# One kernel, one change: eleven instead of six outer products of the first large tile in seven inner ones, with a ring of three buffers for their weight sums and SyncE issuing their stores

## The chip, the cores and the metric

The kernel runs on one core of a Trainium2 chip. The metric is the time of one execution in microseconds (us), measured on the device. A core has TensorE (PE in the profile, with its weight loads as PEld), VectorE (DVE), ScalarE (ACT), GpSimd (POOL) and SyncE (SP), which here issues DMAs only. SPq, ACTq and so on are the engines' instruction queues where they issue a transfer or wait.

## The reference

In float32: an attention without softmax whose scores decay with the distance of the tokens, and a SwiGLU block on its output.

```python
B, H, S, D = 8, 8, 576, 64
scores = (1 / sqrt(D)) * (q @ k.transpose(0, 1, 3, 2))
gamma  = 1 - 2 ** (-5 - h)                           # one for each head h
ret    = (scores * (gamma ** (i - j) where i >= j else 0)) @ v
x      = ret.transpose(0, 2, 1, 3).reshape(B * S, H * D)     # 4608 tokens x 512
g, val = x @ w_gate, x @ w_val                       # 512 x 1536 each
out    = (g * sigmoid(g) * val) @ w_out              # 1536 x 512
```

## The kernel before, in words

**Tiles.** Five token tiles. Tile 0 has 512 tokens and uses plain matmuls (`up0`, `down0`, L853 and L864). Tiles 1 to 4 have 1024 tokens each; each goes through an up stage (`up_stage`, gate and value products, SiLU, hidden values) and a down stage (`down_step`, the product with `w_out`). The attention is cut into ticks, each for one pair of heads of one batch: SyncE loads q, k and v (L282, L287), VectorE transposes and decays (`kT` is one of its results), TensorE forms scores and states (L532, L559 among others), and the output lands transposed in `xs[n]`, the x of the tile. Ticks of the next tiles are mixed into the work of the current one. One load is issued by ScalarE, the last that is recorded before tile 1's up stage (`queue = nc.scalar if i == needed(1) - 3`).

**Fewer multiplications.** The up stage of a large tile goes by three quads `qd` of the hidden size. In each quad, x and the weights are cut 2 x 2, and the block product is formed by seven outer products instead of eight, from sums of blocks (Strassen-Winograd). They are worked in the order `SETS = (1, 2, 6, 7, 4, 5, 3)`. Each outer product is again a 2 x 2 block product and is worked in one of two ways. In the plain one (`whole_slot`) it takes eight inner products; pairs accumulate in PSUM, and four banks are read. In the other one (`slot`) it takes seven inner products and seven reads of a bank, and it needs four inner sums of x (`x_inner`) and four of the weights (`w_inner`). `PLAIN` lists the outer products that are plain, all of tile 1. One inner product is one *slot*: two matmuls of 128 x 256 in `multiply` (L1183), into one of four banks (A, B, C, E). Most reads are VectorE additions in `combine` (L1040), which also is the line of the sums of x and of weights, whichever engine makes them. The outer products 2, 4, 5 and 3 finish hidden values: four `finish` calls each, a SiLU on ScalarE (L1197) and a product (L1198).

**Tile 1** (`busy`) has a second duty: while it runs, GpSimd forms the sums of weights of all 21 outer products, outer (`w_outer`) and inner (`w_inner`). The inner sums go into one of three blocks of SBUF and are stored to `up_sets` in DRAM (L1116); SyncE stores the raw and outer blocks beside them (L1118, L1119). Tiles 2 to 4 fetch them from there (`fetch_one`) and work every outer product in seven. In tile 1, six of the 21 outer products (6 and 7 of each quad) are worked in seven and fifteen are plain: 15 x 8 + 6 x 7 = 162 slots. Its products of L1198 are on VectorE; those of the other large tiles are on GpSimd.

**Order.** Every engine runs its instructions in the order in which they are recorded; nothing reorders them later. In tile 1's up stage a table by hand, `later(at, ...)`, says ahead of which slot a sum or a store is recorded; two loads of q, k and v are recorded after slots 13 and 30, behind a wait of SyncE. The sums of quad 0 that are needed first (`early_sums`) are recorded at the end of tile 0: outer sums 5 and 7 of the weights, inner sums of 1, 2 and 7, and the outer sums of x.

**The output weights.** Their sums (26 operands in each of three quads) are made during tile 0 by `out_sums`: GpSimd for quads 0 and 1 (L886), VectorE for the last. Each operand is stored at once by SyncE (L954) to `dn_ops` in DRAM, and its buffer comes free when the store has read it. They are recorded in groups of three operands; a table in the plan of tile 0 says after which `up0(f)` how many groups follow. The loads of the coming ticks (`next_load`) are recorded between them:

```python
        if f in (7, 10, 11):
            plan.append(lambda t=tick_at[f]: next_load(t))
        for _ in range({7: 3, 10: 4, 11: 3}.get(f, 0)):
            ...
                plan.append(lambda group=groups.pop(0)[1]: group())
```

Of the kernel before, what the change touches and what calls it, by code (L numbers as in the profile page):

```python
# [17 lines left out]
ALU = mybir.AluOpType  # L18
# [88 lines left out]


SETS = (1, 2, 6, 7, 4, 5, 3)
PLAIN = {(1, qd, o) for qd in range(3) for o in (1, 2, 4, 5, 3)}  # L110


def terms(text):
# [18 lines left out]
def kernel(  # L132
# [32 lines left out]
    nc = tc.nc  # L165

    B, H, S, D = q.shape
    NT, DM = out.shape
    DF = moe_w_gate.shape[1]
    P = 128  # L170
# [8 lines left out]
    TB = TW // 4  # L179
    NF = DF // P  # L180
    NQ = NF // 4
# [31 lines left out]
    hid = arena[:, 0 : 3 * QW].rearrange("p (q h t x) -> p q h t x", q=NQ, h=4, t=4)  # L213
# [831 lines left out]
    def x_sets(n):  # L1045

        x = xs[n].rearrange("p (K k) (T t x) -> p T K k t x", k=2, T=2, t=2)
        block = lambda a: rest[:, a : a + 1024].rearrange("p (k t x) -> p k t x", k=2, t=2)
        sets = {1: x[:, 0, 0], 2: x[:, 0, 1], 4: x[:, 1, 1], 7: x[:, 1, 0], 5: block(4096), 6: block(5120), 3: block(x0_at)}
        spots = [rest[:, x0_at + 1024 + TB * i : x0_at + 1024 + TB * (i + 1)] for i in range(4)]  # L1050
        spots += [rest[:, sum_at + 1024 + TB * i : sum_at + 1024 + TB * (i + 1)] for i in range(2)]
        spots += [rest[:, dn_at + 4096 + TB * i : dn_at + 4096 + TB * (i + 1)] for i in range(12)]
        spots += [operands[:, 5376 + TB * i : 5376 + TB * (i + 1)] for i in range(3)]
        new = {o: spots[3 * m : 3 * m + 3] for m, o in enumerate((1, 2, 7, 4, 6, 3, 5) if n == 1 else (1, 2, 7, 4, 5, 3, 6))}
        aside = new[3][2]

        def outer_sums(o, eng):
            a, b, sign = {5: (7, 4, 1), 6: (5, 1, -1), 7: (1, 7, -1), 3: (2, 6, -1)}[o]
            return [lambda k=k: combine(eng, sets[o][:, k], sets[a][:, k], sets[b][:, k], sign) for k in range(2)]

        def inner_sums(o, eng):
            a, (s1, s2, s4) = sets[o], new[o]
            return [lambda: combine(eng, s1, a[:, 0, 1], a[:, 1, 1], 1),
                    lambda: combine(eng, s2, s1, a[:, 0, 0], -1),
                    lambda: combine(eng, aside if o == 1 else a[:, 0, 1], a[:, 0, 0], a[:, 0, 1], -1),
                    lambda: combine(eng, s4, a[:, 1, 0], s2, -1)]

        def put_back(eng):
            a = sets[1]
            return [lambda: combine(eng, a[:, 0, 1], a[:, 0, 0], a[:, 0, 1], -1)]  # L1070

        def view(o, i, qd):
            a, (s1, s2, s4) = sets[o], new[o]
            return {1: a[:, 0, 0], 2: a[:, 1, 0], 3: s4, 4: a[:, 1, 1], 5: s1, 6: s2, 7: aside if o == 1 and qd == 0 else a[:, 0, 1]}[i]

        return outer_sums, inner_sums, put_back, view, sets
# [17 lines left out]
    def w_sets(qd):  # L1094

        up = lambda n, k: w_up[:, qd, :, 2 * n : 2 * n + 2, k, :]
        sets = {1: up(0, 0), 2: up(0, 1), 7: up(1, 0), 3: up(1, 1), 5: hid[:, qd, 2:4, 0:2], 6: hid[:, qd, 0:2, 2:4], 4: hid[:, qd, 2:4, 2:4]}
        blocks = (rest[:, x0_at + 1024 : x0_at + 2048], extra_at(1536, 1024), extra_at(0, 1024))
        new = {o: blocks[b].rearrange("p (g j x) -> p g j x", g=2, j=4) for o, b in {6: 1, 1: 2, 7: 0, 4: 2, 2: 1, 5: 2, 3: 0}.items()}

        def outer_sums(o):
            out, a, b = {5: (5, 7, 1), 6: (6, 3, 5), 7: (7, 3, 7), 4: (4, 2, 6)}[o]
            return [lambda g=g: combine(nc.gpsimd, sets[out][:, g], sets[a][:, g], sets[b][:, g], -1) for g in range(2)]

        def inner_sums(o):
            z = lambda k, m: sets[o][:, :, m, k * P : (k + 1) * P]
            to = lambda j: new[o][:, :, j]
            return [lambda: combine(nc.gpsimd, to(1), z(0, 1), z(0, 0), -1),
                    lambda: combine(nc.gpsimd, to(0), z(1, 1), z(0, 1), -1),
                    lambda: combine(nc.gpsimd, to(2), z(1, 1), to(1), -1),  # L1110
                    lambda: combine(nc.gpsimd, to(3), z(1, 0), to(2), -1)]

        def store(o, new_ones):
            dst = up_sets[qd][SETS.index(o)]
            if new_ones:
                return [lambda: nc.gpsimd.dma_start(out=dst[:, 6 * P :], in_=new[o].rearrange("p g j x -> p (g j x)"))]  # L1116
            raw = dst[:, 0 : 6 * P].rearrange("p (g x) -> p g x", g=2)
            return [lambda: nc.sync.dma_start(out=raw[:, :, P:], in_=sets[o][:, :, 0]),  # L1118
                    lambda: nc.sync.dma_start(out=raw[:, :, 0:P], in_=sets[o][:, :, 1, P:])]  # L1119

        return sets, new, outer_sums, inner_sums, store

    def early_sums():

        x_outer = x_sets(1)[0]
        _, _, w_outer, w_inner, store = w_sets(0)
        p = [w_outer(5), w_inner(1) + store(1, True), w_outer(7), w_inner(2) + store(2, True), w_inner(7) + store(7, True)]
        v = [f for o in (5, 6, 3, 7) for f in x_outer(o, nc.vector)]
        return p, v

    def up_stage(n):

        busy, base = n == 1, used[0]
# [16 lines left out]
        def later(at, *fs):  # L1150
            after.setdefault(at, []).extend(fs)
# [39 lines left out]
        def finish(k, c):  # L1191
            qd, o = seq[k]
            (T, H), (t, h) = final[o], divmod(c - 11, 10)
            src = to(k, c)
            s = io[:, (silus[0] % 4) * TB : (silus[0] % 4 + 1) * TB]
            silus[0] += 1
            nc.scalar.activation(out=s, in_=src[:, 0:TB], func=AF.Silu)  # L1197
            (nc.vector if busy else nc.gpsimd).tensor_tensor(out=hid[:, qd, 2 * H + h, 2 * T + t], in0=src[:, TB : 2 * TB], in1=s, op=ALU.mult)  # L1198

        def made(k, c, at):  # L1200
            if seq[k][1] in final:
# [100 lines left out]
        if not busy:  # L1302
            begin = lambda k: begins[k]
            if n + 1 < NTILE:
                for i, f in enumerate(x_inner(2, nc.gpsimd)):
                    later(i, f)
                for i, f in enumerate(x_outer(7, nc.vector)):
                    later(8 + 2 * i, f)
            for k, o in enumerate((6, 7, 4, 5, 3)):
                for i, f in enumerate(x_inner(o, nc.gpsimd)):  # L1310
                    later(begin(k + 1) - (n + 1 == NTILE) * 3 + i, f)
            later(begin(6), *put_back(nc.gpsimd))
        else:
            for o, at in {6: 6, 7: 10}.items():
                for i, f in enumerate(x_inner(o, nc.gpsimd)):
                    later(at + i, f)
            for qd in range(NQ):
                at = begins[len(SETS) * qd]
                _, _, w_outer, w_inner, store = w_sets(qd)
                if qd:  # L1320
                    outers = {5: 0, 6: 2, 7: 8, 4: 14}
                    inners = {6: 4, 1: 10, 7: 15, 4: 22, 2: 29, 5: 33, 3: 37}
                else:
                    outers, inners = {6: 0, 4: 14}, {6: 2, 4: 18, 5: 27, 3: 37}
                for o, start in outers.items():
                    for i, f in enumerate(w_outer(o)):
                        later(at + start + i, f)
                for o, start in inners.items():
                    for j, f in enumerate(w_inner(o)):
                        later(at + start + j, f)  # L1330
                    later(at + start + 3, *store(o, True))
                for i, o in enumerate((1, 2, 3, 5, 6, 7, 4)):
                    for j, f in enumerate(store(o, False)):
                        later(at + (1, 2, 4, 5, 7, 13, 20)[i] + j, f)

        def go(at):
            for f in after.pop(at, ()):
# [5 lines left out]
            after_tick()  # L1343
            if at % (2 if busy else 3) == 1:
                part_on()
            if busy and at - begins[2 * len(SETS)] in (38, 40, 42):
                fetch_one()
            if at + 1 == len(slots):
                while waiting:
# [102 lines left out]
    for f in range(2, NF):  # L1452
# [7 lines left out]
                plan.append(end_transposes)  # L1460
        if f in (7, 10, 11):
            plan.append(lambda t=tick_at[f]: next_load(t))
        for _ in range({7: 3, 10: 4, 11: 3}.get(f, 0)):
            if f >= (7, 10, NF)[groups[0][0]]:
                if f + 1 == NF and more_places:
                    plan.append(lambda places=more_places[:4]: pool_places.extend(places))
                    more_places.clear()
                if len(groups) % 9 == 0:
                    plan.append(lambda qd=groups[0][0]: negate(qd))
                plan.append(lambda group=groups.pop(0)[1]: group())  # L1470
# [87 lines left out]
```

## Time and profile before

| | |
|---|---|
| time, median of 3 runs | 1034.03 us (1033.91 to 1036.57) |
| profiled execution: time, span | 1034.89 us, 1033.16 us |
| TensorE clock granted, mean | 0.997 |
| PE busy | 1009.1 us, 98% |
| PEld busy | 828.7 us, 80% |
| VectorE busy | 727.6 us, 70% |
| GpSimd busy | 557.4 us, 54% |
| ScalarE busy | 286.7 us, 28% |
| DMA | 194.38 MB, mean 188 GB/s |

By stretches of the span, busy us of each engine:

| from : to | PE | DVE | ACT | POOL | DMA share |
|---|---|---|---|---|---|
| 0 : 178.94 (to the first matmul of tile 1's up stage) | 164.30 | 125.59 | 82.11 | 69.30 | 0.93 |
| 178.94 : 337.26 (tile 1's up stage) | 153.66 | 125.06 | 42.39 | 105.64 | 0.69 |
| 337.26 : 1033.00 (the rest) | 691.11 | 476.90 | 162.22 | 382.47 | 0.58 |

How to read it: times in the profile are microseconds from the start of the span, of one execution. An engine's busy time leaves out register and branch instructions, semaphores, and the issuing of DMAs; where an engine issues DMAs, that time is in its queue's rows. A row `PE bankA L1183 <- DVE rest L1040` is idle time of PE ahead of a matmul into bankA, ended by a VectorE instruction of L1040.

### The profile page before, as it was taken

The page shows a single profiled execution, that of the slowest core. Times are in us where ns is not written, and L with a number is a line of the kernel's source. Part 1 is how long each engine was busy: PE and PEld are TensorE (multiplying, and loading weights), DVE is VectorE, ACT ScalarE, POOL GpSimd, SP SyncE. Part 2 cuts the span into 40 slices and gives each one's busy share as a digit, 9 for nine tenths or more (in the row PEclk, how much of TensorE's full clock was granted, in tenths as well). Part 3 has the DMA queues.
Part 4 walks back from the last instruction along what each step waited for, and adds up shares of the span by engine and source line. Part 5 has one row for each costly group of instructions (what it writes and reads, how often), then busy time and mean ns, then how long its engine had stood idle before and what let it go on. Part 6 is the DMA issues. An engine that isn't in the chain of part 4 may idle for free.

```text
span 1033.2 us, 21382 instructions
## 1 busy us (share of the span) xinstructions
PE 1009.1 (98%) x8356; PEld 828.7 (80%) x8356; DVE 727.6 (70%) x1212; ACT 286.7 (28%) x638; POOL 557.4 (54%) x603
## 2 busy tenths in 40 slices
PE   6999989998999999999999999999999999999998
PEld 4644445887888888888888888888888888888887
DVE  5488878587788766875768768858576668565744
ACT  4465532131242231123333111133220012333110
POOL 3402259867474216764657237765582486566625
PEclk9999999999999999999999999999999999999999
DMA  9999887856595887756558777443454554445553
GB/s 242 251 263 248 216 198 264 262 147 191 116 260 159 203 237 197 208 178 181 166 163 234 197 187 218 163 144 143 143 189 154 159 162 163 154 142 182 177 162 102
DMA packets 281612, 194.38 MB, mean 188 GB/s; under 512 B 212968, under 2 KB 251112, under 8 KB 281512
## 3 DMA queue, kind: packets, MB, share of 16 engines
q1 hardware_dynamic: 244088, 82.51, 32.9%
q10 hardware_dynamic: 33760, 99.10, 29.2%
q0 software_dynamic: 3664, 11.41, 3.0%
q8 instruction: 66, 1.08, 0.5%
q14 instruction: 34, 0.28, 0.1%
HBM read 154.04 MB, written 38.93 MB: 187 GB/s over the span
## 4 chain that ended last, share of the span: by engine, by line
PE 82%; DMA 7%; DVE 5%; SPq 2%; issue 1%; ACT 1%; POOL 1%; ACTq 0%; DVEq 0%; POOLq 0%
PE bankE L1183 11%; PE bankA L1183 11%; PE bankB L1183 10%; PE bankC L1183 10%; PE bankB L1374 7%; PE bankC L1374 7%; PE bankE L1374 7%; PE bankA L1374 6%; DVE rest L1040 2%; PE outer L1183 2%; PE inner L1183 2%; PE outer L532 1%; DMA v<-in_v_dram 1%; PE outer L559 1%; DMA dn<-rest 1%
## 5 line engine op out<-in xcount | busy, mean ns | idle before, releaser
L1040 POOL TENSOR_TENSOR rest<-rest 128x512 f32<-128x512 f32 (+1 forms) x141 | 150.4, 1078 | 156.6 <-DVE rest L1040 114.2
L1198 POOL TENSOR_TENSOR arena<-rest,io 128x256 f32<-128x256 f32 x144 | 105.7, 745 | 73.2 <-ACT io L1197 72.9
L1197 ACT ACTIVATE io<-rest 128x256 f32<-128x256 f32 x192 | 79.4, 417 | 219.6 <-DVE rest L1040 159.2
L1183 PE MATMUL bankA<-rest,arena 128*128 128x256 f32 x416 | 107.6, 384 | 4.1 <-DVE rest L1040 3.9
L1183 PE MATMUL bankB<-rest,arena 128*128 128x256 f32 x416 | 106.1, 380 | 0.1
L1040 DVE TENSOR_TENSOR rest<-bankB,rest 128x512 f32<-128x512 f32 x113 | 76.1, 682 | 38.5 <-PE bankB L1183 24.6
L1183 PE MATMUL bankE<-rest,arena 128*128 128x256 f32 x400 | 102.2, 380 | 0.3 <-issue 0.3
L1040 DVE TENSOR_TENSOR rest<-bankA,rest 128x512 f32<-128x512 f32 x106 | 71.5, 682 | 40.6 <-PE bankA L1183 21.0
L1040 DVE TENSOR_TENSOR rest<-bankE,rest 128x512 f32<-128x512 f32 x105 | 71.0, 684 | 38.7 <-PE bankE L1183 25.8
L1040 POOL TENSOR_TENSOR arena<-arena 128x256 f32<-128x256 f32 (+1 forms) x84 | 76.3, 929 | 34.7 <-PE bankC L1183 19.6
L1183 PE MATMUL bankC<-rest,arena 128*128 128x256 f32 x372 | 94.8, 380 | 0.1
L1183 PEld LDWEIGHTS bankA<-rest,arena 128*128 128x128 f32 x416 | 78.8, 191 | 17.1 <-issue 3.4
L1040 DVE TENSOR_TENSOR rest<-bankC,rest 128x512 f32<-128x512 f32 x103 | 69.7, 683 | 30.1 <-PE bankC L1183 12.6
L1183 PEld LDWEIGHTS bankB<-rest,arena 128*128 128x128 f32 x416 | 78.8, 190 | 11.6 <-DVE rest L1040 0.9
L1183 PEld LDWEIGHTS bankE<-rest,arena 128*128 128x128 f32 x400 | 75.3, 190 | 11.8 <-DVE rest L1040 0.8
L1183 PEld LDWEIGHTS bankC<-rest,arena 128*128 128x128 f32 x372 | 70.1, 190 | 10.8 <-DVE rest L1040 1.2
L886 POOL TENSOR_TENSOR rest<-rest 128x256 f32<-128x256 f32 x43 | 34.3, 822 | 74.3 <-DVE rest L407 38.8
L1374 PE MATMUL bankB<-arena 128*128 128x256 f32 x264 | 61.0, 381 | 0.0
L1374 PE MATMUL bankC<-arena 128*128 128x256 f32 x264 | 60.8, 380 | 0.0
L1374 PEld LDWEIGHTS bankC<-arena 128*128 128x128 f32 x264 | 50.0, 190 | 6.9
L1374 PEld LDWEIGHTS bankB<-arena 128*128 128x128 f32 x264 | 49.8, 190 | 6.9
L1374 PE MATMUL bankA<-arena 128*128 128x256 f32 x240 | 55.3, 380 | 0.0
(267 smaller groups left out, 1930.1 us busy)
## 6 DMA issues: line engine op xcount, KB each, us to landing
arena<-up ACTq DMA_DIRECT2D x63, 896.0 KB, 4.6
arena<-dn ACTq DMA_DIRECT2D x65, 384.0 KB, 3.7
arena<-dn SPq DMA_DIRECT2D x39, 384.0 KB, 3.4
dn<-rest SPq DMA_DIRECT2D x78, 128.0 KB, 1.8
out_dram<-rest SPq DMA_DIRECT2D x35, 256.0 KB, 3.1
qk<-in_q_dram SPq DMA_DIRECT2D x108, 72.0 KB, 2.8
qk<-in_k_dram SPq DMA_DIRECT2D x108, 72.0 KB, 3.5
up<-arena POOLq DMA_DIRECT2D x15, 512.0 KB, 4.3
```

Of the source, the lines that this page charges most:

```text
L532: m = nc.tensor.matmul(value(i, hl, c), s["v"][rows, at], ret[rows, c % 2 if whole(i) else hl, c // 2], start=start, stop=start, skip_grou ...
L559: nc.tensor.matmul(xr[half[hl]] if c + 1 == NC else value(i, hl, c), state[half[hl], c, :], s["qT"][half[hl], ts(c, L)], start=False, stop ...
L886: eng.tensor_tensor(out=dst, in0=srcs[0], in1=srcs[1], op=ALU.add if op[0] == "add" else ALU.subtract)
L1040: eng.tensor_tensor(out=out, in0=a, in1=b, op=ALU.add if sign > 0 else ALU.subtract)
L1183: m = nc.tensor.matmul(b[:, g * TB : (g + 1) * TB], w[:, g], x, start=(opens and g == 0), stop=True, skip_group_check=True)
L1197: nc.scalar.activation(out=s, in_=src[:, 0:TB], func=AF.Silu)
L1198: (nc.vector if busy else nc.gpsimd).tensor_tensor(out=hid[:, qd, 2 * H + h, 2 * T + t], in0=src[:, TB : 2 * TB], in1=s, op=ALU.mult)
L1374: nc.tensor.matmul(b[:, m * TB : (m + 1) * TB], lhs[:, qd, ts(m, P)], w[:, qd], start=(opens and qd == 0 and m == 0), stop=(qd == NQ - 1), ...
```

## The change

Each part changes only the order, the engine or the buffer of work, and five outer products of tile 1.

- `PLAIN`: five more outer products of tile 1 are worked in seven inner ones: product 2 of quad 0, and products 1 and 2 of quads 1 and 2. Six become eleven, 162 slots become 157.
- `x_sets`, `w_sets`: other buffers for the inner sums. The three blocks of weight sums are used in turn, one ring over all 21 products.
- `store`: SyncE issues the stores of the inner weight sums in place of GpSimd.
- `early_sums`: the inner weight sums of product 7 are no longer recorded ahead of the stage.
- `finish`: in tile 1, the hidden products of outer product 2 go to GpSimd.
- `up_stage`: new slots for the sums and stores; the inner sums of product 1 of the next quad are made at slot 42 of the quad before. The fetches of the first output-weight operands move two slots ahead.
- the plan of tile 0: three of the ten groups of output-weight sums, which were recorded after `up0(7)`, are recorded after `up0(10)`, behind the `next_load` there.

```diff
-PLAIN = {(1, qd, o) for qd in range(3) for o in (1, 2, 4, 5, 3)}
+PLAIN = {(1, qd, o) for qd in range(3) for o in (1, 2, 4, 5, 3) if qd == 0 and o == 1 or o in (4, 5, 3)}
...
-        new = {o: spots[3 * m : 3 * m + 3] for m, o in enumerate((1, 2, 7, 4, 6, 3, 5) if n == 1 else (1, 2, 7, 4, 5, 3, 6))}
-        aside = new[3][2]
+        new = {o: spots[3 * m : 3 * m + 3] for m, o in enumerate((4, 5, 1, 2, 6, 7, 3) if n == 1 else (1, 2, 7, 4, 5, 3, 6))}
+        aside = new[3][2] if n > 1 else sets[1][:, 0, 1]
...
-        blocks = (rest[:, x0_at + 1024 : x0_at + 2048], extra_at(1536, 1024), extra_at(0, 1024))
-        new = {o: blocks[b].rearrange("p (g j x) -> p g j x", g=2, j=4) for o, b in {6: 1, 1: 2, 7: 0, 4: 2, 2: 1, 5: 2, 3: 0}.items()}
+        blocks = (extra_at(0, 1024), extra_at(1536, 1024), rest[:, x0_at + 1024 : x0_at + 2048])
+        new = {o: blocks[(qd + i) % 3].rearrange("p (g j x) -> p g j x", g=2, j=4) for i, o in enumerate(SETS)}
...
-                return [lambda: nc.gpsimd.dma_start(out=dst[:, 6 * P :], in_=new[o].rearrange("p g j x -> p (g j x)"))]
+                return [lambda: nc.sync.dma_start(out=dst[:, 6 * P :], in_=new[o].rearrange("p g j x -> p (g j x)"))]
...
-        p = [w_outer(5), w_inner(1) + store(1, True), w_outer(7), w_inner(2) + store(2, True), w_inner(7) + store(7, True)]
+        p = [w_outer(5), w_inner(1) + store(1, True), w_outer(7), w_inner(2) + store(2, True)]
...
-            (nc.vector if busy else nc.gpsimd).tensor_tensor(out=hid[:, qd, 2 * H + h, 2 * T + t], in0=src[:, TB : 2 * TB], in1=s, op=ALU.mult)
+            (nc.vector if busy and o != 2 else nc.gpsimd).tensor_tensor(out=hid[:, qd, 2 * H + h, 2 * T + t], in0=src[:, TB : 2 * TB], in1=s, op=ALU.mult)
...
-            for o, at in {6: 6, 7: 10}.items():
+            for o, at in {2: 0, 6: 10, 7: 18, 1: 28}.items():
                 for i, f in enumerate(x_inner(o, nc.gpsimd)):
                     later(at + i, f)
...
-                    outers = {5: 0, 6: 2, 7: 8, 4: 14}
-                    inners = {6: 4, 1: 10, 7: 15, 4: 22, 2: 29, 5: 33, 3: 37}
+                    outers, inners = {5: 4, 6: 6, 7: 12, 4: 18}, {2: 0, 6: 8, 7: 14, 4: 20, 5: 27, 3: 34}
                 else:
-                    outers, inners = {6: 0, 4: 14}, {6: 2, 4: 18, 5: 27, 3: 37}
+                    outers, inners = {6: 4, 4: 22}, {6: 6, 7: 14, 4: 24, 5: 32, 3: 37}
...
+                if qd + 1 < NQ:
+                    *_, next_inner, next_store = w_sets(qd + 1)
+                    for j, f in enumerate(next_inner(1)):
+                        later(at + 42 + j, f)
+                    later(at + 45, *next_store(1, True))
                 for i, o in enumerate((1, 2, 3, 5, 6, 7, 4)):
                     for j, f in enumerate(store(o, False)):
-                        later(at + (1, 2, 4, 5, 7, 13, 20)[i] + j, f)
+                        later(at + (1, 2, 4, 8, 10, 15, 25)[i] + j, f)
...
-            if busy and at - begins[2 * len(SETS)] in (38, 40, 42):
+            if busy and at - begins[2 * len(SETS)] in (36, 38, 40):
                 fetch_one()
...
-        for _ in range({7: 3, 10: 4, 11: 3}.get(f, 0)):
+        for _ in range({10: 7, 11: 3}.get(f, 0)):
```

## The prediction

> **What bounds the kernel now.** I read the page's chain first, then TensorE's waits by stage, then the chain, the granted clock and each engine's timeline inside tile 1's up stage, the only stage that the change rewrites.
>
> ```profile
> PE 82%; DMA 7%; DVE 5%; SPq 2%; issue 1%; ACT 1%; POOL 1%; ACTq 0%; DVEq 0%; POOLq 0%
> ```
>
> TensorE carries 82% of the chain that ends last, so a cut pays where it leaves the PE queue without a gap. The second view is PE's waits from 140 to 350 us (total, times, longest), the third the chain there (start, length).
>
> ```profile
> PE bankA L1183 <- DVE rest L1040: 3.5, 3, 3.1
> PE outer L532 <- ACT rest L626: 2.6, 1, 2.6
> ```
> ```profile
> 238.53 4.98 DVE arena L1198
> 245.19 2.04 PE bankA L1183 x4
> ```
>
> The reader is to see that the stage's longest PE wait, 3.1 us, comes from a VectorE product (L1198) that took 5 us, and that PE then needs 2.04 us for four matmul records. The VectorE and GpSimd timelines and the windows around it (columns: PE, PEld, DVE, ACT, POOL busy, granted clock, DMA share, GB/s) say why:
>
> ```profile
> 238.45 5.06 DVE L1198 TENSOR_TENSOR arena<-rest,io 128x256 f32<-128x256 f32 x1
> ...
> 244.04 0.41 DVE L1198 TENSOR_TENSOR arena<-rest,io 128x256 f32<-128x256 f32 x1
> ```
> ```profile
> 242.20:245.20 3.00, 0.01 (x1) 0.04 (x1) 3.00 (x5) 0.42 (x1) 2.60 (x5) 0.97 1.10 362
> 245.20:248.90 3.70, 3.70 (x72) 2.83 (x72) 3.38 (x4) 0.00 (x0) 3.30 (x6) 0.56 0.60 222
> ```
>
> The same instruction takes 0.41 us when GpSimd pauses and 5.06 us beside an unbroken run of GpSimd sums; after the PE gap the granted clock is 0.56.
>
> The stage runs from 178.94 to 337.26, 158.3 us: 162 inner products, each 0.8635 us from start to start, are 139.9; four attention ticks of about 2.3 and one half tick of 1.0 are 10.2; 8.2 is lost. Of that the stop at 242 costs 5.1 (3.07 idle, the rest slow clock: the bankB matmuls at 249.90 would have begun at 244.8), 1.2 a gap at 284 with no releaser, about 1.1 small gaps at 303 to 312.
>
> **Fewer inner products.** Five outer products, (quad 0, set 2), (1,1), (1,2), (2,1), (2,2), go from eight inner products to seven: 5 x 0.8635 = **-4.3 us**, all on the PE path. The order of instructions confirms it: 157 instead of 162.
>
> **The set-2 products move from VectorE to GpSimd.** Twelve L1198. In before these twelve are the ones that start from 190.16 to 195.47, 236.79 to 245.57 and 296.16 to 303.83; they took 2.5 + 7.7 + 6.9 = 17.1 us of VectorE, the 5.06 included. Five more products on the seven-way path add 15 VectorE reads of a bank at 0.60 from start to start, 9.0 us. VectorE is relieved by 8 us, and the stop at 242 loses its cause: **-5.1 us**. Bounds: nothing, if another product is caught, or all 5.1.
>
> [...] The row is a slow clock after 3.07 us of idleness. [...]
>
> **GpSimd.** Removed: 21 store issues at 0.58 plus the 0.30 wait ahead of each, 18.4 us. Added: eight sums of x (0.75) and twelve products (0.745), 14.9 us. The total falls, but the order tightens, because PE now needs the sums at once. Two things decide.
>
> First, when GpSimd reaches this work. Three groups of output-weight sums (L886) are recorded behind a load that they preceded, and their stores share SyncE with it:
>
> ```profile
> 118.28 8.27 SPq L954 DMA_DIRECT2D dn<-rest  x9
> 126.65 2.05 SPq L282 DMA_DIRECT2D qk<-in_q_dram  x4
> ```
> ```profile
> 122.20 5.38 POOL L886 TENSOR_TENSOR rest<-rest 128x256 f32<-128x256 f32 x6 [20.88 <-DMA dn<-rest]
> ...
> 167.80 7.02 POOL L1040 TENSOR_TENSOR arena<-arena 128x512 f32<-128x512 f32 x6
> 175.12 0.58 POOL L1116 DMA_DIRECT2D up<-arena  x1 [0.30 <-POOL arena L1040]
> 175.72 5.67 POOL L1040 TENSOR_TENSOR arena<-arena 128x512 f32<-128x512 f32 x6
> ```
>
> Before, nine stores go at 118.28 and GpSimd, out of buffers, resumes at 122.20. Now the load goes first: it can start at 122.2 (the end of the transpose that frees its buffer) and lasts 5.9 (126.65 to 132.58), so the first store leaves at 128.1, 9.8 later, and GpSimd resumes at 132.0. Forty sums remain, at 0.89 (31 in 27.5 us up to 167.8): 167.5, plus 3.2 of the waits for stores seen from 147 to 167. So 170.7 instead of 167.8, **2.9 later**; bounds 0 and 9.8.
>
> Second, the queue of quad 0. From 170.7: weight sums for sets 5, 1, 7, 2 (7.02 + 5.67, no store) to 183.4; x sums of set 2 (3.1) 186.5; weight sums of set 6 (2.6 + 3.0) 192.1; x sums of 6 (3.1) 195.2; four of set 2's products (0.73 each) among the weight sums of 7 (3.0) and x sums of 7 (3.1), which start at 200.4 and end at 203.5; the last product 204.2; weight sums of 4 (2.6) 206.8. PE asks, slot s being at 178.94 + 0.8635 s: x sum 1 of set 6 at slot 15, 191.9, ready 192.8, 0.9 late; x sum 1 of set 7 at slot 22, 197.9 + 0.9, ready 201.2, 2.4 more; set 4's sum at slot 27, 202.3 + 3.3, ready 206.8, 1.2 more. **+4.5 us** of new PE waits on GpSimd. With GpSimd 2.9 earlier the same sums give 1.6, and 9.8 late 11.4.
>
> **VectorE in quads 1 and 2.** Each now opens with 28 inner products of the seven-way kind instead of 14, where a bank is read every 0.86 us and four banks leave little slack. 24 reads x 0.60 = 14.4 plus two ticks of 3.9 are 22 of some 29 us, without the four products left over from set 3. The like stretch of before, 303 to 312 us, lost 1.1 in 14 slots with one tick; four such stretches in place of that one: 4.4 - 1.1 = **+3.3 us**; bounds 0 and 7.
>
> **Stores on SyncE, ring of three.** 21 issues at some 0.5 us are 10.5 us of a queue that waits 51.6 us in this window for VectorE's kT; behind a store that waits for its sums stand the raw-weight stores and the next q, k, v load. The load issued at 259.76 is transposed at 276.09, so about 10 us cover it: 0; with the cover gone, what exceeds it falls on a tick. A buffer comes round after three sets, some 18 us of PE, against 4.3 us to land: 0.
>
> **A wait ahead of tile 1.** ScalarE's v load (L287) issues at 138.88 and holds the copies behind it, and PE loses 2.65 at 142.8 plus 2 on a slow clock. In the new order it waits for the seventh output-weight store instead of its own queue's k load. That store leaves at 128.1 + 4.8 or, if held by the k loads' landing, near 137, and lands 1.8 to 3.9 later: 134.7 to 141. Value 0, bounds -4 and +2.
>
> **The sum.** -4.3 - 5.1 + 4.5 + 3.3 = -1.6. The profiled execution took 1034.89 (span 1033.16), 0.86 above the median of 1034.03. On the profile 1033.3, on the median **1032.4 us**. PE has 0.7 us of waits after 350, so a shift of the stage reaches the end.
>
> **Rivals.** A: GpSimd is not late, since its work to 167.8 is mostly paced by 0.4 us store issues and more buffers come free before the regrouped sums; then quad 0 costs 1.6 and the ScalarE wait shrinks by about 2: -1.6 - 2.9 - 2 = -6.5, 1027.5. For it: GpSimd idles 33 us from 101 to 149; against: all its 46 sums still follow one queue. B, slower: the moved load delays the sums in full. GpSimd's last L886 then ends at 177.6, quad 0 costs 11.4, and the time is 1039.3; it makes the change a loss once that end passes 172.3 (170.7 + 1.6). For it: every wait of GpSimd there names dn stores; against: the stall of 10.7 at 129.6 is absorbed. C: the lock moves. Set 3's products now fall in the next quad's seven-way product; one took 2.86 at 289.64. Two such waits of 2 give back 4: +2.4, 1036.4.
>
> [...]
>
> **How the numbers follow.** The forecast has 0.42, A 0.24, B 0.20, C 0.14. About 0.3%, 3.1 us, is what can be told from no change. Faster by more: 0.36 of the forecast's 0.42 and nearly all of A, 0.37. Slower by more: most of B, a third of C, 0.24. Same 0.39. The range runs from below A, 1026.5, to short of B's full price, 1038.5; the forecast's own is 1029 to 1036.
>
> **What would show it.** Right: no L1183 wait near 242 and no L1198 above 3 us on VectorE; PE waits on POOL L1040 between 190 and 207 totalling about 4.5; GpSimd's first arena sum near 170.7; the stage near 156.7 us. Wrong: PE waits for POOL beyond 8 us (B), a stage under 153 (A), PE waiting behind L1198 again in quads 1 or 2 (C), or the first L1183 more than 2 us from 178.94.

## The result, and the profile after

The changed kernel takes 1026.62 us (median of 9 runs, 1024.85 to 1028.60); the kernel before took 1034.03 (9 runs, 1027.78 to 1038.49). The ratio is 0.9935, 95% interval 0.9914 to 0.9956: faster by 7.4 us on the medians, where 1.6 was forecast. 1026.62 is inside the stated range of 1026.5 to 1038.5 by 0.1 us and outside the forecast's own 1029 to 1036. The profiled execution took 1026.62, span 1024.9, so it stands at the median.

The three stretches of the span, before and after: to the first L1183 178.94 and 175.69 us; tile 1's up stage 158.32 and 152.99; the rest 695.9 and 696.2. First the row of the stage (columns: from and to, length, PE, PEld, DVE, ACT, POOL busy, clock, DMA share, GB/s), then the chain's shares by engine and PE's waits from 140 to 350 us (total, times, longest), all of the changed kernel.

```profile
175.69:328.68 152.99, 148.96 (x1241) 127.83 (x1240) 110.81 (x198) 42.97 (x105) 109.81 (x133) 1.00 0.72 203
```
```profile
PE 69%; DVE 2%; issue 1%; SPq 0%; DMA 0%; DVEq 0%; ACT 0%
```
```profile
PE outer L567 <- DVE kT L492: 1.5, 1, 1.5
PE bankE L1183 <- ACT rest L869: 0.9, 1, 0.9
PE bankA L1183 <- POOL rest L1040: 0.9, 1, 0.9
PE bankB L1183 <- DVE rest L1040: 0.9, 1, 0.9
PE bankB L1183 <- ACT rest L1228: 0.6, 1, 0.6
...
PE bankC L1183 <- POOL arena L1040: 0.3, 1, 0.3
```

The chain can be followed only in part here (its shares add up to 72%), so the waits are the better view. The one stop of 3.1 us is gone; in its place stand seven small ones (one of 0.3 and one of 0.2 are left out), none with a slow clock behind it: the granted clock of the stage is 1.00. L567 lies ahead of the stage. One wait was in no sum: 0.9 for ScalarE's copy of tile 0's output (L869), ahead of which ScalarE stood idle for 3.58, up to 181.45, behind a store of output weights (`DMA dn<-rest`). The order ahead of the stage is in SyncE's and GpSimd's timelines:

```profile
120.31 2.97 SPq L282 DMA_DIRECT2D qk<-in_q_dram  x4
...
127.37 53.22 SPq L954 DMA_DIRECT2D dn<-rest  x78
```
```profile
132.01 0.72 POOL L886 TENSOR_TENSOR rest<-rest 128x256 f32<-128x256 f32 x1 [12.05 <-DMA dn<-rest]
...
168.43 12.89 POOL L1040 TENSOR_TENSOR arena<-arena 128x512 f32<-128x512 f32 x12
```

The first output-weight store leaves at 127.37 (forecast 128.1), GpSimd resumes at 132.01 (forecast 132.0), and all 78 stores now follow the load. GpSimd's first sum for tile 1 begins at 168.43 (167.80 before, 170.7 forecast), 7.3 us ahead of the first L1183; before it was 11.1.

### The profile page after: what moved, and what is told of

It is laid out like the page before. It is cut to its first block, busy times and chain, and to the rows that moved or that the text cites. A ratio compares the mean times of both kernels' runs of the same rounds, so it can differ in the third digit from the quotient of the medians.

```text
span 1024.9 us, 21387 instructions
## 1 busy us (share of the span) xinstructions
PE 1003.7 (98%) x8336; PEld 823.0 (80%) x8336; DVE 713.3 (70%) x1215; ACT 286.3 (28%) x638; POOL 557.5 (54%) x602
## 4 chain that ended last, share of the span: by engine, by line
PE 69%; DVE 2%; issue 1%; SPq 0%; DMA 0%; DVEq 0%; ACT 0%
PE bankC L1183 9%; PE bankB L1183 9%; PE bankA L1183 9%; PE bankE L1183 9%; PE bankB L1378 7%; PE bankE L1378 7%; PE bankC L1378 7%; PE bankA L1378 6%; PE outer L1183 2%; PE inner L1183 2%; DVE rest L1040 2%; PE outer L532 1%; PE outer L559 1%; PE inner L573 1%; PE inner L543 1%
## 5 line engine op out<-in xcount | busy, mean ns | idle before, releaser
L1198 POOL TENSOR_TENSOR arena<-rest,io 128x256 f32<-128x256 f32 x156 | 113.8, 740 | 88.6 <-ACT io L1197 83.2
L1183 PE MATMUL bankB<-rest,arena 128*128 128x256 f32 x448 | 114.9, 381 | 1.0 <-DVE rest L1040 0.9
L1183 PE MATMUL bankA<-rest,arena 128*128 128x256 f32 x412 | 105.4, 381 | 1.4 <-POOL rest L1040 0.9
L1183 PE MATMUL bankC<-rest,arena 128*128 128x256 f32 x416 | 106.4, 380 | 0.4 <-DVE rest L1040 0.2
L1183 PEld LDWEIGHTS bankB<-rest,arena 128*128 128x128 f32 x448 | 84.5, 190 | 13.8 <-POOL rest L1040 1.2
L1183 PE MATMUL bankE<-rest,arena 128*128 128x256 f32 x372 | 95.0, 380 | 0.4 <-DVE rest L1040 0.3
L1183 PEld LDWEIGHTS bankA<-rest,arena 128*128 128x128 f32 x412 | 77.7, 190 | 13.6 <-DVE rest L1040 1.8
L1183 PEld LDWEIGHTS bankC<-rest,arena 128*128 128x128 f32 x416 | 78.3, 190 | 12.6 <-DVE rest L1040 1.4
L1183 PEld LDWEIGHTS bankE<-rest,arena 128*128 128x128 f32 x372 | 69.9, 190 | 11.7 <-DVE rest L1040 1.6
L1378 PE MATMUL bankE<-arena 128*128 128x256 f32 x264 | 60.8, 380 | 0.0
L1378 PEld LDWEIGHTS bankE<-arena 128*128 128x128 f32 x264 | 49.9, 190 | 6.9
L886 POOL TENSOR_TENSOR arena<-arena 128x768 f32<-128x768 f32 x24 | 47.0, 1961 | 15.3 <-DVE arena L1198 14.7
```

Of the source, the lines that this page charges most:

```text
L886: eng.tensor_tensor(out=dst, in0=srcs[0], in1=srcs[1], op=ALU.add if op[0] == "add" else ALU.subtract)
L1183: m = nc.tensor.matmul(b[:, g * TB : (g + 1) * TB], w[:, g], x, start=(opens and g == 0), stop=True, skip_group_check=True)
L1198: (nc.vector if busy and o != 2 else nc.gpsimd).tensor_tensor(out=hid[:, qd, 2 * H + h, 2 * T + t], in0=src[:, TB : 2 * TB], in1=s, op=ALU ...
L1378: nc.tensor.matmul(b[:, m * TB : (m + 1) * TB], lhs[:, qd, ts(m, P)], w[:, qd], start=(opens and qd == 0 and m == 0), stop=(qd == NQ - 1), ...
```

## The experiments

Each kernel was timed beside the kernel before on the same chip; its medians there were 1033.58 (the two single parts and the two reversals that come first), 1034.41 (the next four) and 1032.83 (the last four), so small differences between groups are read from the ratios. "First L1183" and "stage" are from one profiled execution each. "Set-2 products" are the twelve hidden products (L1198) of outer product 2 in tile 1; the last three kernels of the table are told further down.

| kernel | median us | ratio to before, 95% | first L1183 | stage us |
|---|---|---|---|---|
| before | 1034.03 | | 178.94 | 158.32 |
| changed | 1026.62 | 0.9935 (0.9914 to 0.9956) | 175.69 | 152.99 |
| before + groups moved | 1036.85 | 1.0036 (1.0015 to 1.0057) | 178.11 | 163.85 |
| before + set-2 products on GpSimd | 1026.97 | 0.9937 (0.9914 to 0.9961) | 176.86 | 152.46 |
| before + stores on SyncE | 1026.08 | 0.9915 (0.9883 to 0.9947) | 180.14 | 151.69 |
| changed, groups back | 1022.86 | 0.9896 (0.9872 to 0.9921) | 174.51 | 150.36 |
| changed, set-2 products on VectorE | 1026.59 | 0.9943 (0.9916 to 0.9970) | 177.95 | 151.67 |
| changed, stores on GpSimd | 1038.11 | 1.0041 (1.0020 to 1.0061) | 174.74 | 165.43 |
| changed, groups back, set-2 on VectorE | 1023.02 | 0.9900 (0.9869 to 0.9932) | 174.71 | 149.98 |
| the same again, other chip | 1025.25 | 0.9926 (0.9898 to 0.9953) | 176.47 | 149.89 |
| changed, five products plain again | 1029.11 | 0.9949 (0.9929 to 0.9969) | 176.79 | 154.62 |
| before + stores on SyncE, one-column issues | 1086.77 | 1.0527 (1.0487 to 1.0568) | 181.53 | 217.40 |
| before + stores on SyncE, filler copies | 1027.44 | 0.9947 (0.9922 to 0.9972) | 177.23 | 152.36 |
| changed, groups back, set-2 on VectorE, v load on SyncE | 1023.10 | 0.9907 (0.9877 to 0.9938) | 174.51 | 151.05 |

**The groups alone, in the kernel before.**

```diff
-        for _ in range({7: 3, 10: 4, 11: 3}.get(f, 0)):
+        for _ in range({10: 7, 11: 3}.get(f, 0)):
```

> The kernel before with one part of the change, the three groups of output-weight sums recorded after up0(10) instead of up0(7). Theory 1 (the regrouping moved the work ahead of tile 1's up stage): the waits of PE at 104.85 (1.52, behind the SiLU) and at 142.80 (2.65) shrink as in the changed kernel, the first L1183 comes near 175.7 instead of 178.94, and the median is some 3 us below the kernel before. Theory 2 (those 3.2 us are the swing from one execution to the next): the first L1183 stays within 1 us of 178.9 and the median within 1 us of the kernel before.

Neither: 3.3 us slower. PE's waits in its stage:

```profile
PE bankB L1183 <- POOL rest L1040: 3.9, 1, 3.9
PE bankA L1183 <- DVE rest L1040: 3.8, 3, 3.1
```

The old stop of 3.1 is still there, and a new one of 3.9 behind GpSimd, whose first sum for tile 1 came at 170.24, 7.9 us ahead of the first L1183 instead of 11.1. So regrouping makes GpSimd some 3.3 us late, as forecast, and that is what it costs.

**The set-2 products alone, in the kernel before.**

```diff
-            (nc.vector if busy else nc.gpsimd).tensor_tensor(out=hid[...
+            (nc.vector if busy and o != 2 else nc.gpsimd).tensor_tensor(out=hid[...
```

> The kernel before with one part of the change, the products of outer product 2 in tile 1 on GpSimd instead of VectorE. Theory 1 (the stop at 242 comes from these products and is in most executions): no L1198 above 3 us on VectorE, no PE wait near 242, a stage of 153 to 154.5 us instead of 158.3, and a median 4 to 5 us below the kernel before. Theory 2 (the stop is an accident of the profiled execution, or another product is caught in its place): a stage above 156.5 us and a median within 1.5 us of the kernel before.

The stop is gone, the stage is 152.46, and the median falls by 6.6, somewhat more than theory 1 priced: theory 1, and almost the whole result of the change from one line. But the next two say that this line isn't what the changed kernel lives on.

**The changed kernel with the groups back, and with the set-2 products back on VectorE** (the two diffs above, reversed).

> The changed kernel with the three groups back after up0(7). Theory 1: the first L1183 goes back to about 178.9, PE waits before it return, the wait of 0.93 at 182 for ScalarE's copy (L869) goes, because the last output-weight stores land earlier, and GpSimd reaches tile 1's sums earlier relative to PE, which removes the 1.2 us of waits on it; in all 1 to 2.5 us above the changed kernel. Theory 2: the first L1183 stays near 176 and the median within 0.7 us of the changed kernel.

> The changed kernel with the products of outer product 2 back on VectorE. Theory 1: VectorE products beside GpSimd's sums take 1.5 to 5 us again in quads 1 and 2, where four banks are read in turn without slack, and PE stops behind them: 3 to 6 us above the changed kernel. Theory 2 (the fewer inner products alone made the gain): within 1.5 us of the changed kernel, PE waits under 2 us at 230 to 310, and quad 0 even gains the 1.2 us that PE now waits for GpSimd.

With the groups back it is 3.8 us faster, where one theory had it slower and the other level: neither. The first L1183 comes at 174.51, GpSimd leads by 10.7 us again, and the waits for L869 and for the bankB read are gone, while two for GpSimd stay:

```profile
PE bankA L1183 <- POOL rest L1040: 0.7, 1, 0.7
...
PE bankC L1183 <- POOL arena L1040: 0.3, 1, 0.3
```

With the set-2 products back on VectorE nothing is lost (1026.59), and no L1198 on VectorE takes more than 1.48 us: theory 2 in the time, and against my account of the stop. Something else in the change keeps VectorE's products short. Row by row, the six long products of the kernel before (over 1.9 us) all start during a store issue of GpSimd or within 2.2 us of its end, which led to the next experiments.

**The stores alone, in the kernel before, and the changed kernel without them.**

```diff
-                return [lambda: nc.gpsimd.dma_start(out=dst[:, 6 * P :], ...
+                return [lambda: nc.sync.dma_start(out=dst[:, 6 * P :], ...
```

> The kernel before with one part of the change, SyncE instead of GpSimd issuing the stores of the inner weight sums. Theory S (a GpSimd run of sums that follows one of its own store issues keeps a VectorE product out until the run's first gap; without such issues a product is let in at the next boundary of two sums): no L1198 on VectorE above 1.6 us, no stop of PE near 242, a stage of 151 to 154 us instead of 158.3, and a median 5 to 8 us below the kernel before. Theory P (the stop comes from where the products of outer product 2 stand, and the stores are free): the 5 us product and the stop stay, and the median is within 2 us of the kernel before.

> The changed kernel with GpSimd issuing the stores of the inner weight sums again. Theory S: L1198 on VectorE above 2 us are back (none in the changed kernel), and with them and 21 issues of 0.9 us on GpSimd's queue (0.58 and the 0.30 ahead of it) PE waits on GpSimd in quad 0; 4 to 10 us above the changed kernel. Theory P: L1198 stays below 1.6 us since the set-2 products are off VectorE, and only the issues cost, 2 to 3 in quad 0: 1 to 4 us above the changed kernel.

Theory S both times, with 0.3 and 1.5 us more than it priced, and one product of 1.72 us at the stage's end where it allowed 1.6. One line gives 8.3 us; taken out of the changed kernel it costs 11.5. Not all of the 11.5 is VectorE's: GpSimd's queue is longer by its issues (21 of 0.58 us, with 0.30 ahead of each), and PE waits 4.5 us for it in quad 0, against 1.2 in the changed kernel. VectorE's and GpSimd's timelines where the stop had been, first of the kernel before with stores on SyncE:

```profile
238.60 1.42 DVE L1198 TENSOR_TENSOR arena<-rest,io 128x256 f32<-128x256 f32 x1
...
240.55 0.89 DVE L1198 TENSOR_TENSOR arena<-rest,io 128x256 f32<-128x256 f32 x1
```
```profile
233.16 8.00 POOL L1040 TENSOR_TENSOR arena<-arena 128x512 f32<-128x512 f32 x8
```

then of the changed kernel with stores on GpSimd:

```profile
228.57 5.57 DVE L1198 TENSOR_TENSOR arena<-rest,io 128x256 f32<-128x256 f32 x1
```
```profile
228.33 0.58 POOL L1116 DMA_DIRECT2D up<-rest  x1 [0.30 <-POOL rest L1040]
228.92 7.67 POOL L1040 TENSOR_TENSOR arena<-arena 128x512 f32<-128x512 f32 x7
```

Both products run beside sums of GpSimd that the view joins to one run, 8.00 and 7.67 us long. The one without an issue ahead is done after 1.42 us, 0.3 after the end of the sum that it met; the one that starts during an issue is done only after 5.57, and PE then waits 4.1 us.

**Neither the groups nor the move of the products.**

> The changed kernel with two parts undone: the three groups back after up0(7), and the products of outer product 2 back on VectorE. Theory S: neither part is needed once SyncE issues the stores; PE's waits on GpSimd in quad 0 (0.68 and 0.31 with the groups alone put back) go as well, so 1020.5 to 1023, at or below the 1022.9 of the kernel with the groups alone put back. Theory P: the products stop PE again, 1025 to 1028.

Theory S, at its upper end: 1023.02, level with the 1022.86 of the groups alone put back, and PE no longer waits for GpSimd in the stage. Once SyncE issues the stores, moving twelve products to GpSimd is worth nothing that can be measured here.

**The five outer products plain again.**

```diff
-... for o in (1, 2, 4, 5, 3) if qd == 0 and o == 1 or o in (4, 5, 3)}
+... for o in (1, 2, 4, 5, 3)}
...
-            for o, at in {2: 0, 6: 10, 7: 18, 1: 28}.items():
+            for o, at in {6: 10, 7: 18}.items():
```

> The changed kernel with the five outer products plain again, so 162 slots, and without the inner sums of x that they needed. By the count of slots alone 4.3 us above the changed kernel. Theory 1 (waits of PE for GpSimd and for VectorE's reads give back about half of it): 1.5 to 3 us above, with the waits at 187 to 203 and at 270 to 286 gone. Theory 2 (the five products are worth their whole 4.3): 3.5 to 5 us above.

2.5 us slower on the medians, 1.4 by the ratios (the two intervals overlap), 1.6 in the stage, of 4.3 by the count: nearer to theory 1, with about half of it or more given back. The waits at 187 to 203 are gone, as expected, and in quads 1 and 2 only 0.2 of waits on VectorE stays. But a gap of 1.5 us at 280 that no instruction ended is back, like the 1.1 of the kernel before at 284, which the count leaves out.

**Is it the issue, or the time that it takes?** Two kernels, both the kernel before with the stores on SyncE. In one GpSimd also issues a transfer of one column at each place; in the other it does a copy there.

```diff
+                        lambda: nc.gpsimd.dma_start(out=mark[qd * 7 + SETS.index(o)], in_=new[o][:, 0, 3, 0:1])]
```
```diff
+                        lambda: nc.gpsimd.tensor_copy(out=fill, in_=new[o][:, :, 3])]
```

> The kernel before with SyncE issuing the stores of the inner weight sums, and at each of those places GpSimd additionally issues a transfer of one column (512 bytes) of the same sums to a DRAM scratch that nothing reads. The store itself is on SyncE, only GpSimd's issue is back. Theory S (GpSimd's issue is what keeps VectorE's product out until the next gap): L1198 of 2 us and more are back behind the issues, with a stop of PE in quad 1 or 2, and most of the 8 us that SyncE's stores gained is lost: 1031 to 1037. Theory T (the path or the landing of the 512 KB stores counts): no L1198 above 1.6 us, 1024 to 1028.

> The kernel before with SyncE issuing the stores of the inner weight sums, and at each of those places GpSimd does a copy of 128x256 to a scratch buffer that nothing reads, so that its queue is about as long as with its own issues and has a gap in the same place, but no issue. Theory S: no L1198 above 1.8 us, no stop of PE by VectorE in quad 1 or 2, 1025 to 1028. Theory Q (the 18 us of issues only moved GpSimd's sums against VectorE's products, and any filler does it): L1198 above 2 us and a stop are back, 1030 to 1036.

The filler kernel took 1027.44, 5.4 us below the kernel before, and no product is caught: apart from one of 1.72 beside GpSimd's sums of 1.8 at the stage's end, none in the stage takes more than 1.2 us. That is theory S. Around the place of the old stop (L1200 is the product's line, L1118 the copy's):

```profile
236.74 0.74 DVE L1200 TENSOR_TENSOR arena<-rest,io 128x256 f32<-128x256 f32 x1
...
238.47 0.43 DVE L1200 TENSOR_TENSOR arena<-rest,io 128x256 f32<-128x256 f32 x1
```
```profile
235.49 0.47 POOL L1118 COPY fill<-arena 128x256 f32<-128x256 f32 x1
235.93 2.68 POOL L1041 TENSOR_TENSOR arena<-arena 128x512 f32<-128x512 f32 x2
```

The kernel with one-column issues has the long products back:

```profile
237.46 4.68 DVE L1200 TENSOR_TENSOR arena<-rest,io 128x256 f32<-128x256 f32 x1
```
```profile
236.31 0.56 POOL L1118 DMA_DIRECT2D mark<-rest  x1 [0.29 <-POOL rest L1041]
236.89 8.19 POOL L1041 TENSOR_TENSOR arena<-arena 128x512 f32<-128x512 f32 x8
```

Its time, 1086.77, missed the expectation by 50 us for another reason: beside the tiny transfers the 512 KB stores took 13.2 us to land instead of 3.7, GpSimd waited 79 us for its buffers and ScalarE stood idle for 29 us ahead of an issue of its own. Only its products say something, and they agree with theory S. What the filler leaves open: the copy took 0.40 to 0.47, about half of an issue with the wait ahead of it (0.58 and 0.30), so GpSimd's queue was not quite as long.

**A load moved off ScalarE.** The groups-back, set-2-on-VectorE kernel, with and without

```diff
-                    queue.dma_start(out=dst.rearrange("p (g d) -> p g d", d=D), in_=tokens(src, b, p))
+                    (nc.sync if dst is t else queue).dma_start(out=dst.rearrange(...
```

> The changed kernel with the groups back after up0(7) and the set-2 products back on VectorE, and the v transfer of the load that ScalarE issues (L287) put on SyncE, so that ScalarE's copies no longer stand behind its wait. Theory W (that wait, 0 to 2.7 us of PE and a slow clock behind it, is most of the swing of 174.5 to 180 in the first L1183): no PE wait on ScalarE's L626 near 139, the first L1183 at 173 to 175, and a median 0.5 to 2 us below the same kernel without this edit, 1021 to 1022.5. Theory D (SyncE brings v too late behind the output-weight stores, or the swing comes from the loads before 100 us): PE waits for v at 150 to 165, or no difference within 0.5 us.

> The changed kernel with the groups back after up0(7) and the set-2 products back on VectorE, a second time, to compare with on the same chip and for a second profile: 1022 to 1024, a stage of 150 us, a first L1183 between 174.5 and 178.

1023.10 with it and 1025.25 without, on one chip; the intervals overlap, and both missed what was expected (1021 to 1022.5 and 1022 to 1024). The first L1183 came at 174.51 and 176.47, and with the edit PE has no wait at all from 95 to 176. But its partner had no wait for L626 either; what it had were 0.8 behind kT, 0.5 behind a SiLU and 0.5 behind L857. Inconclusive.

## Why the prediction was off: right in direction, a fifth of the size

**The step that failed is "Stores on SyncE, ring of three", 0.** It weighed SyncE's queue and GpSimd's time and let nothing of VectorE's depend on who issues. Measured alone it is -8.3 us on the medians and -6.6 in the stage; the 5.1 of the stop at 242, which the forecast gave to the set-2 products, is part of that. The rows to see it were in the trace of the kernel before: the 5.06 at 238.45 starts inside the store issue of 238.09 to 238.67, and the other five long products of that stage stand behind an issue likewise. GpSimd's timeline there:

```profile
238.09 0.58 POOL L1116 DMA_DIRECT2D up<-arena  x1 [0.30 <-POOL arena L1040]
238.69 2.50 POOL L1040 TENSOR_TENSOR arena<-arena 128x512 f32<-128x512 f32 x2
241.14 1.41 POOL L1040 TENSOR_TENSOR rest<-arena 128x256 f32<-128x256 f32 x2
242.50 1.59 POOL L1040 TENSOR_TENSOR rest<-arena,rest 128x256 f32<-128x256 f32 x2
```

**"The stop at 242 loses its cause", -5.1.** The stop went and brought what was priced, but its cause was named one step short. "Beside an unbroken run of GpSimd sums" is half of it. Removing the products from VectorE removes the stop (-6.6 alone), and so does removing the issues (-8.3 alone); the second makes the first worth nothing (1026.62 and 1026.59; 1022.86 and 1023.02). The runs of the kernel before spread over 10.7 us, those of the changed kernel over 3.8; that its other executions have such stops elsewhere would fit, but only one of them was profiled.

**GpSimd late by 2.9.** The lateness is right: over the profiles its first sum for tile 1 begins at 167.8 to 170.2 with the groups moved and at 163.8 to 167.8 without, and its lead on the first L1183 is 7.0 to 8.6 us against 9.2 to 13.9. The price went another way than forecast. PE's waits on GpSimd, put at 4.5, are 1.2 in the changed kernel and still 1.0 with the groups back; what else goes with the groups is 0.9 behind L869 and 0.9 behind a bank's read, neither of them in the sum. So it is luck that the step's whole cost is close to the forecast's 2.9 (4.5 less the 1.6 that quad 0 costs without it): 2.6 in the stage, 3.8 on the medians against the kernel with the groups back. Elsewhere the groups cost 3.3 (kernel before) and 3.6 or 1.3 (set-2 products on VectorE, by which of the two measurements is taken). Rival B's mechanism, a loss by the moved load, is in the runs at well under half of its price (3.8 against 11.4 - 1.6 = 9.8).

**Five products, -4.3, and VectorE in quads 1 and 2, +3.3.** The count holds, 157 slots; the waits were priced too high. The gaps of PE in quads 1 and 2 add up to 1.5 (0.3, 0.7 and 0.5 ahead of the matmuls at 271.19, 283.31 and 286.51, the second of them behind a copy of ScalarE), where the +3.3 stands for 4.4 less the 1.1 that the kernel before loses: 0.4 net, inside the bounds. With quad 0's 1.6 the forecast makes these terms +0.6 together; the runs make them -1.6 in the stage and -2.5 on the medians. This is about as large a part of the miss as what the stores give beyond the 5.1 of the stop.

**The wait ahead of tile 1, 0.** The stage began 3.25 us earlier, which the prediction gave as a sign against itself. The regrouping isn't the reason: over the profiles the first L1183 lies from 174.7 to 178.1 with the groups moved and from 174.5 to 181.5 without. This is the swing of one execution, and so is ScalarE's wait (L626), 0.9 us here instead of 2.6: it is 0 to 1.7 over the profiles with the groups moved and 0 to 2.7 without.

**The sum by the runs:** stores -8.3, five products -2.5, groups +3.8, products' move 0: -7.0, against -7.4 measured; in the stage -6.6 - 1.6 + 2.6 = -5.6, against -5.3. Each term is uncertain by some us, so the agreement is no proof. That the range just holds the result is luck: it reached down to 1026.5 for rival A. A had the number, 1027.5, and its sign, a stage under 153 us (152.99), but not the mechanism, since GpSimd is late; rival C, the stop moving to other products, didn't happen in the changed kernel, and does with the stores on GpSimd: the 5.57 at 228.57 is one of the products left on VectorE. The change is faster by the line that the prediction priced at nothing, and one of its parts costs half as much as the whole gains: with the groups put back it takes 1022.86, the shortest median here, or 1023.02 and 1025.25 without the products' move.

## What to carry to other kernels

Where a VectorE instruction takes many times its usual time beside GpSimd (here 5.06 us instead of 0.41), look at what GpSimd did just before its run of sums, not only at the run; if it is a DMA issue, try another engine's queue first (here worth 8.3 us). Price an edit to who issues a transfer also by the engines beside it, and test parts alone: two remedies for one stop needn't add up (here 6.6 and 8.3 us alone, and 1026.62 in the changed kernel, which has both, against 1026.59 without the first). A part that only "makes room" for the others, here the regrouping (3.8 us), can be the one to leave out.

## What the runs showed of the hardware that was not expected

In tile 1's up stages a VectorE product of L1198 (0.41 us beside an idle GpSimd, at 206.51 in the kernel before) that met GpSimd's sums took 1.72 us at most when no DMA issue of GpSimd stood ahead of them. When one did, about every second product that started near it was done only when GpSimd's sums came to their first gap. Counted row by row over tile 1's up stages and the 6 us behind them, of 216 such products in the five profiles with GpSimd's issues 28 took more than 1.9 us, up to 5.57, and all 28 started between 0.4 us before the end of an issue and 2.4 after it, a stretch in which 55 of the 216 started; of 395 in nine profiles without, none did (longest 1.72). All 28 ended 0.3 us after the last sum ahead of GpSimd's first gap, which was 0.08 us long in 21 of them, ahead of a sum that needs the one just before it. Why an issue has this effect, and why on only half of these products, no run here shows.

One 128x512 sum of GpSimd (1.28 us, at 216.53 in the kernel before) and the product's own 0.41 make 1.7, an estimate from these two rows. The longest product of the nine profiles without issues, 1.72, is close to it; the 5.06 and 5.57 of the five with issues are about three times as long.

Beside GpSimd's transfers of one column (128 rows of 4 bytes) most others landed later: from 175 to 345 us the 512 KB stores on SyncE took 13.2 us (median) instead of 3.7 without them, the 256 KB ones 9.5 instead of 3.4, the loads of v 12.6 instead of 4.0; the loads of `kn` stayed at 3.5. One kernel shows this, and nothing here says why.
